# Attention and two feed-forward blocks in fp32: P*V of two heads on one half of the TensorE columns each, with the row sums taken by products of their own

## The chip, the cores and the metric

The kernel runs on one core of a Trainium2 chip. Its time is the device time of one execution in microseconds (us); of several runs the median counts. The engines are TensorE (PE, its weight loads shown as PEld), VectorE (DVE), ScalarE (ACT), GpSimd (POOL) and the DMA queues, which SyncE (SP), ACT and POOL issue.

## The reference

Three stages, all in fp32: attention with a soft cap on the scores, a feed-forward block with a sigmoid gate, and a second one with an RMS norm and a SiLU gate.

```
batch, n_heads, seq, head_dim = (2, 12, 448, 64)

def _attn_ref(q, k, v, cap):
    scores = q @ k.T / sqrt(64)
    scores = cap * tanh(scores / cap)
    attn = exp(scores - max(scores))
    attn = attn / (sum(attn) + 1e-09)
    return attn @ v

x = attention, as 896 tokens x 768
x = moe (x, w_in 768x2048, w_out 2048x768)
x = moe2(x, rms_g, w_gate and w_val 768x1536, w_out 1536x768)
```

The change touches the last two lines of the attention alone: the sum over the keys, its reciprocal, and the product with V.

## The kernel before, in words

**Pairs.** The 24 heads are worked off as 12 pairs (p, 0 to 11) of two heads each (e, 0 and 1). The 448 keys of a head are three chunks of 128 and a rest of 64. Scores are made transposed, with the keys on the partitions: for chunk c, `scores` (L296) writes a tile `s` with both heads side by side, six products of 64 contraction rows, three for each head, in the order e = 0, 1, 0, 1. The rests of both heads share one tile of 128 partitions (`scores_last`, L306, with the block weights `kb`). `exps` (L318, L319) applies tanh and exp on ACT and leaves the unnormalized P of a chunk in SBUF: `tt` (128x896, both heads) for a chunk and `tl` (128x448) for the rests. No maximum is subtracted.

**P*V and the sums.** `pv(p, e)` (L330) runs once for each head: four fp32 products (three chunks and the rest), each with 128 weight columns. 64 of these are the head's V, and the other 64 are ones, which POOL writes into the tiles `vn` and `ve` at the start. So one PSUM bank receives the output on one half of its partitions and the row sum, repeated, on the other. DVE copies the bank into `z` (L336; for the last pair ACT does, L338).

**The reciprocals.** `sums` cuts one row of each head's `z` over 64 partitions by a DMA (L344, into `rs`, 128x7), `recips` inverts these 128x7 numbers on DVE (L350) and writes them to DRAM (L353, `recs`), and `spread` reads them back over all partitions (L368, `r`, 128x448). All three are DMAs that POOL issues. For the last three pairs the DMA from `z` is issued by SP, and the spreading is done on chip, with a product by a pattern `spr` on DVE (L358) and a product with block weights `blk` on PE (L372). `norm_mul` (L379, once for each head, 64 partitions), `norm_hi` (L385; ACT for the last two pairs, L387) and `norm_lo` (L391) write the normalized output as a high and a low part into `x`, the feed-forward block's input.

**The order.** The program is written out by hand: each engine works in the order of the calls in the loop `for p in range(NPR + 1)`. Iteration p of it issues, on PE: scores of chunk 1 of pair p (L296); transposes of q and k of pair p + 1 (L264); P*V of head 0 of pair p - 1; scores of chunk 2 of p and of chunk 0 of p + 1; `scores_last`; P*V of head 1 of pair p - 1. Between these stand DVE's copy and split of the transposed q and k (L274, L275), POOL's copies into `kb` (L277), the reciprocals of pair p - 3, and the normalization of pair p - 4 (`normal`). `decode` sprinkles in three steps per iteration, from iteration 3 on, of the unpacking of the first feed-forward weights (on DVE L137, L143, L149, L163; on ACT L125, L129, L133, L158): one step behind the first P*V, two behind the normalization. After the loop the first feed-forward block begins (`ffn1`, products at L541 to L543). Its first three columns of 18 products use tokens of the first batch alone (pairs 0 to 5); the tokens of pairs 6 to 11 are read first by the 128x512 products that follow.

**PSUM.** The attention has two tiles `s` of two banks, one `t` of two banks for the transposes, and two banks `v`, which warm-up, `scores_last` and P*V take in turn: whoever takes one waits until the reader of the use before last is done.

Of the kernel before, what the change touches and what calls it, by code (L numbers as in the profile page):

```python
# [18 lines left out]
def attn_moe_kernel(  # L19
# [14 lines left out]
    nc = tc.nc  # L34
# [22 lines left out]
    spr = keep.tile([128, S], F32, name="spr")  # L57
# [119 lines left out]
    def attention():  # L177
        with ExitStack() as actx:
# [15 lines left out]
            vns = [ap_.tile([128, NC, 12 - 4 * i, D], F32, name=f"vn{i}", bufs=1) for i in range(2)]  # L194
            ves = [ap_.tile([128, 3 - i, 4, D], F32, name=f"ve{i}", bufs=1) for i in range(2)]
            kbs = [ap_.tile([128, 2, 128], F32R, name=f"kb{i}", bufs=1) for i in range(2)]

            def constants():
                for r in raws:
                    for nm in "kq":  # L200
                        nc.gpsimd.memset(r[nm][64:128, NC], 0.0)
                for kb in kbs:
                    nc.gpsimd.memset(f(kb), 0.0)
                for vn, ve in zip(vns, ves):
                    for c in range(NC):
                        nc.gpsimd.memset(vn[:, c, 1::2], 1.0)
                    for e in range(2):
                        nc.gpsimd.memset(ve[half[e], :, 1 + e], 1.0)
                        nc.gpsimd.memset(ve[half[1 - e], :, 2 * e:2 * e + 2], 0.0)

            def late_constants():
                for e in range(2):
                    nc.gpsimd.memset(spr[half[e]], 1.0)
                    for lo in (True, False):

                        nc.gpsimd.affine_select(
                            out=spr[half[e]], in_=spr[half[e]], pattern=[[1 if lo else -1, S]],
                            compare_op=ALU.is_ge, fill=0.0, base=0 if lo else 6,
                            channel_multiplier=-7 if lo else 7,
                        )  # L220
# [3 lines left out]
            xs, pt, zt, nr = {}, {}, {}, {}  # L224
# [12 lines left out]
            def load_v(g):  # L237
                p0, n = GROUPS[g]
                for c in range(NC):
                    nc.sync.dma_start(  # L240
                        out=vns[g % 2][:, c, 0:4 * n:2], in_=rows(v, p0, n, c).rearrange("h p d -> p h d")
                    )
                for e in range(2):
                    nc.sync.dma_start(
                        out=ves[g % 2][half[e], 0:n, 3 * e], in_=rows(v, p0, n, NC)[e:2 * n:2].rearrange("h p d -> p h d")
# [76 lines left out]
            def pv(p, e):  # L322

                g, i = place[p]
                h = 2 * i + e
                ps = ps_v.tile([128, 512], F32, tag="v", name="v")
                for c in range(NC + 1):

                    w = vns[g % 2][:, c, 2 * h - e:2 * h - e + 2] if c < NC else ves[g % 2][:, i, 2 * e:2 * e + 2]
                    nc.tensor.matmul(  # L330
                        out=ps[:, 0:S], lhsT=w.rearrange("p h d -> p (h d)"),
                        rhs=pt[p, c][:, e] if c < NC else pt[p, c], start=(c == 0), stop=(c == NC),
                    )
                zt[p, e] = zrp.tile([128, S], F32, tag="z", name="z", bufs=7)
                if p < NPR - 1:
                    nc.vector.tensor_copy(zt[p, e], ps[:, 0:S])  # L336
                else:
                    nc.scalar.activation(out=zt[p, e], in_=ps[:, 0:S], func=AF.Copy)  # L338

            def sums(p):  # L340
                nr[p] = zrp.tile([128, S // 64], F32, tag="rs", name="rs", bufs=3)
                for e in range(2):

                    (nc.gpsimd if p < NPR - 3 else nc.sync).dma_start(  # L344
                        out=nr[p][half[e]], in_=zt[p, e][64 - 64 * e:65 - 64 * e, :].rearrange("o (a n) -> o a n", a=64)
                    )

            def recips(p):
                rs = nr[p]
                nc.vector.reciprocal(out=rs, in_=rs)  # L350
                if p < NPR - 3:
                    d = dram.tile([2, S], F32, tag="recs", name="recs")
                    nc.gpsimd.dma_start(out=d.rearrange("e s -> (e s)").rearrange("(p n) -> p n", p=128), in_=rs)  # L353
                    nr[p] = d
                else:

                    r = zrp.tile([128, S], F32, tag="r", name="r", bufs=3)
                    nc.vector.tensor_tensor(  # L358
                        out=r.rearrange("p (a n) -> p a n", n=7), in0=spr.rearrange("p (a n) -> p a n", n=7),
                        in1=rs.unsqueeze(1).to_broadcast([128, 64, 7]), op=ALU.mult,  # L360
                    )
                    nr[p] = r

            def spread(p, bank=None):
                d = nr[p]
                if p < NPR - 3:
                    r = zrp.tile([128, S], F32, tag="r", name="r", bufs=3)
                    nc.gpsimd.dma_start(out=r, in_=d.unsqueeze(1).to_broadcast([2, 64, S]))  # L368
                    nr[p] = (r, r)
                else:  # L370
                    o = bank()
                    nc.tensor.matmul(out=o[:, 0:S], lhsT=blk, rhs=d, start=True, stop=True)  # L372
                    nr[p] = (o[:, 0:S], d)

            def norm_mul(p):
                by, r = nr[p]
                for e in range(2):
                    z = zt.pop((p, e))
# [473 lines left out]
```

## Time and profile before

| | |
|---|---|
| Median of 3 runs | 640.83 us (640.73 to 641.07) |
| Span of the profiled execution, first to last instruction | 639.5 us |
| PE, DVE, ACT, POOL busy, share of the span | 98%, 69%, 63%, 13% |
| Attention, to the first feed-forward product | 138.5 us |

The profile lists each execution of an instruction with its engine, line and tiles. "Span" runs from the first to the last instruction; the time of a run holds some 1.3 us more. No other time of the profiled execution is shown. A busy PE is not a PE at its peak, since records of products overlap: the distance between starts tells more than their length. L296 is line 296 of the kernel before, which is printed above.

### The profile page before, as it was taken

Reading aid. Unit: us, or ns where it says so; the run is one execution under the profiler, and the core shown is the slowest. Engines: PE = TensorE matmul, PEld = TensorE weight load, DVE = VectorE, ACT = ScalarE, POOL = GpSimd, SP = SyncE. Lnnn points to the kernel's source line nnn. Section 1 sums busy time; section 2 is a strip of 40 time slices with the busy share of each in tenths; the row PEclk is TensorE's granted clock in tenths of the full one; section 3 lists DMA queues with packets and bytes.
Section 4 is the critical chain, followed back from the end, with each engine's and each line's share of the span. In section 5 each row is a group of like instructions: output and inputs, shape, how many; then the busy total and the mean of one; then the engine's idle time right before and its main releaser. Section 6 shows DMA issues by size and latency. Waiting matters only on the chain.

```text
span 639.5 us, 8022 instructions
## 1 busy us (share of the span) xinstructions
PE 627.8 (98%) x3076; PEld 529.1 (83%) x3076; DVE 439.0 (69%) x561; ACT 400.4 (63%) x534; POOL 81.1 (13%) x127
## 2 busy tenths in 40 slices
PE   7999999988999999999999999999999999999997
PEld 4655555557888899899898888999998899999997
DVE  2235677667777554467678889999378887588842
ACT  4869878828777654677767666668345676355500
POOL 5322233200000000000002220310012200023100
PEclk9999999999999999999999999999999999999999
DMA  6836433133423442233333423434323234232012
GB/s 136 184 97 149 120 79 97 31 87 89 134 100 121 127 147 82 68 99 106 132 109 98 127 73 102 144 100 148 99 63 134 101 100 148 58 137 102 1 64 109
DMA packets 85925, 67.18 MB, mean 105 GB/s; under 512 B 39924, under 2 KB 83206, under 8 KB 85888
## 3 DMA queue, kind: packets, MB, share of 16 engines
q1 hardware_dynamic: 80720, 64.28, 33.1%
q0 software_dynamic: 4208, 2.16, 1.3%
q8 instruction: 24, 0.39, 0.3%
q10 hardware_dynamic: 960, 0.23, 0.2%
q14 instruction: 13, 0.11, 0.1%
HBM read 63.80 MB, written 2.78 MB: 104 GB/s over the span
## 4 chain that ended last, share of the span: by engine, by line
PE 92%; DVE 3%; DMA 3%; issue 1%; SPq 1%; ACT 1%; POOL 0%; ACTq 0%; DVEq 0%; POOLq 0%
PE b L543 21%; PE b L542 21%; PE b L541 21%; PE b L746 14%; PE v L330 8%; PE s L296 4%; PE t L264 2%; PE v L306 1%; DMA r<-recs 1%; DMA q<-in_q 1%; DVE r L379 1%; SPq L235 1%; DMA rs<-z 0%; DVE x L274 0%; DVE x L391 0%
## 5 line engine op out<-in xcount | busy, mean ns | idle before, releaser
L541 PE MATMUL b<-x,ring 128*128 128x512 f32 (+1 forms) x480 | 174.4, 363 | 0.0
L543 PE MATMUL b<-x,ring 128*128 128x512 f32 (+1 forms) x480 | 174.2, 363 | 0.0
L542 PE MATMUL b<-x,ring 128*128 128x512 f32 (+1 forms) x480 | 174.0, 363 | 0.0
L542 PEld LDWEIGHTS b<-x,ring 128*128 128x128 f32 x480 | 90.1, 188 | 10.2 <-issue 0.4
L541 PEld LDWEIGHTS b<-x,ring 128*128 128x128 f32 x480 | 90.1, 188 | 10.1 <-issue 0.4
L543 PEld LDWEIGHTS b<-x,ring 128*128 128x128 f32 x480 | 90.1, 188 | 9.4
L746 PE MATMUL b<-ring,uA 128*128 128x384 f32 x504 | 87.8, 334 | 0.0
L746 PEld LDWEIGHTS b<-ring,uA 128*128 128x128 f32 x504 | 87.4, 188 | 0.0
L137 DVE SCALAR_TENSOR_TENSOR dec<-raw,dec 128x768 uint32<-128x768 uint32 x68 | 69.7, 1024 | 24.6 <-ACT dec L133 23.2
L143 DVE SCALAR_TENSOR_TENSOR dec<-raw,dec 128x768 uint32<-128x768 uint32 x68 | 73.1, 1076 | 1.1
L543 PE MATMUL b<-g,ring 128*128 128x384 f32 (+1 forms) x192 | 70.0, 365 | 0.0
L542 PE MATMUL b<-g,ring 128*128 128x384 f32 (+1 forms) x192 | 69.8, 364 | 0.0
L541 PE MATMUL b<-g,ring 128*128 128x384 f32 (+1 forms) x192 | 69.6, 362 | 0.0
L163 DVE TENSOR_TENSOR ring<-dec,ring 128x768 fp32r<-128x768 f32 x68 | 66.7, 983 | 3.6 <-ACT ring L158 3.6
L158 ACT ACTIVATE ring<-dec 128x768 fp32r<-128x768 f32 x68 | 56.7, 834 | 16.7 <-DVE dec L149 8.5
L149 DVE SCALAR_TENSOR_TENSOR dec<-raw,dec 128x768 uint32<-128x768 uint32 x68 | 64.9, 954 | 1.3
L129 ACT ACTIVATE dec<-dec,edge 128x768 f32<-128x768 f32 x68 | 63.4, 932 | 0.9
L125 ACT ACTIVATE dec<-raw 128x768 f32<-128x768 f32 x68 | 60.8, 894 | 0.6 <-DVE ring L163 0.5
L133 ACT ACTIVATE dec<-dec 128x768 f32<-128x768 f32 x68 | 57.3, 842 | 1.5
L330 PE MATMUL v<-tt,vn 128*128 128x448 f32 x144 | 58.2, 540 | 0.0
L714 POOL TENSOR_TENSOR a<-a,gg 128x512 f32<-128x512 f32 (+1 forms) x18 | 29.7, 1648 | 188.6 <-DVE gg L707 188.6
L318 ACT ACTIVATE tt<-s,tsc 128x896 f32<-128x896 f32 x36 | 35.9, 997 | 19.5 <-PE s L296 19.5
(103 smaller groups left out, 666.7 us busy)
## 6 DMA issues: line engine op xcount, KB each, us to landing
raw<-in_moe_w_out SPq DMA_DIRECT2D x20, 768.0 KB, 4.2
raw<-in_moe_w_in SPq DMA_DIRECT2D x16, 768.0 KB, 4.6
raw<-in_moe_w_gate SPq DMA_DIRECT2D x12, 768.0 KB, 4.2
raw<-in_moe_w_val SPq DMA_DIRECT2D x12, 768.0 KB, 4.2
raw<-in_moe_w_out SPq DMA_DIRECT2D x8, 512.0 KB, 3.8
out<-oacc SPq DMA_DIRECT2D x6, 384.0 KB, 2.3
raw<-in_moe_w_out SPq DMA_DIRECT2D x8, 256.0 KB, 3.6
r<-recs POOLq DMA_DIRECT2D x9, 224.0 KB, 7.7
```

Of the source, the lines that this page charges most:

```text
L125: nc.scalar.activation(out=f(d), in_=f(r[:, :, 1]), func=AF.Square, scale=2.0 ** 15)
L129: nc.scalar.activation(out=f(d), in_=f(d), func=AF.Sign, bias=edge)
L133: nc.scalar.activation(out=f(d), in_=f(d), func=AF.Relu, scale=2.0 - 2.0 ** -23)
L137: nc.vector.scalar_tensor_tensor(out=d, in0=hi, scalar=3, in1=d, op0=ALU.logical_shift_left, op1=ALU.bitwise_and)
L143: nc.vector.scalar_tensor_tensor(out=d, in0=hi, scalar=0xC0000000, in1=d, op0=ALU.bitwise_and, op1=ALU.bitwise_or)
L149: nc.vector.scalar_tensor_tensor(out=d, in0=lo, scalar=29, in1=d, op0=ALU.logical_shift_right, op1=ALU.bitwise_or)
L163: nc.vector.tensor_tensor(out=t[:, 1], in0=f(d), in1=f(t[:, 0]), op=ALU.subtract)
L330: nc.tensor.matmul(out=ps[:, 0:S], lhsT=w.rearrange("p h d -> p (h d)"), rhs=pt[p, c][:, e] if c < NC else pt[p, c], start=(c == 0), stop= ...
L541: nc.tensor.matmul(out=wide(o, b), lhsT=w0, rhs=x0, start=first, stop=False)
L542: nc.tensor.matmul(out=wide(o, b), lhsT=w0, rhs=x1, start=False, stop=False)
L543: nc.tensor.matmul(out=wide(o, b), lhsT=w1, rhs=x0, start=False, stop=last)
L746: nc.tensor.matmul(out=os_[t][n][:, 0:HW], lhsT=uA[xi][:, i, tok], rhs=w[:, wi, n * HW:(n + 1) * HW], start=(i == 0 and xi == 0 and wi == ...
```

## The change

Line numbers of the kernel after are those of its own text (its P*V is L314 and L318, its products for the sums L341 and L345).

- `outputs(p)` takes the place of the two `pv`. The tiles `vn` and `ve` hold V alone. For each of three chunks there are two products of 64 weight columns: head 0 into PSUM partitions 0 to 63, head 1 into 64 to 127 of the same bank. The rest of both heads is one product of 128 columns with block weights `ve`. One copy (L324) moves the bank to `z`; the last pair's is ACT's.
- `add_two` (DVE, L330) and `add_third` (POOL, L333) add the three tiles `tt` of a pair into `ts` (128x896). `sums` multiplies `ts` with ones, 64 columns for each head, and `tl` with `blk`, into one more bank. The last pair has no `ts`: its three `tt` are multiplied one by one.
- Up to pair 8 DVE copies the sums' bank to `sc` (L350), and the way over the DMAs is that of before. For pairs 9, 10 and 11 DVE inverts the bank, 128x448, straight from PSUM (L358). `spr`, its pattern, `bank`, the product with `blk` behind it and SP's DMAs are gone.
- `norm_mul` is one instruction of 128 partitions instead of two of 64. `normal(9)` moves to the end of iteration 11, `normal(10)` into iteration 12's end, behind `sums`; pair 11 is normalized in the first feed-forward step.

```diff
-            def pv(p, e):
+            def outputs(p):
                 g, i = place[p]
-                h = 2 * i + e
                 ps = ps_v.tile([128, 512], F32, tag="v", name="v")
-                for c in range(NC + 1):
-                    w = vns[g % 2][:, c, 2 * h - e:2 * h - e + 2] if c < NC else ves[g % 2][:, i, 2 * e:2 * e + 2]
-                    nc.tensor.matmul(
-                        out=ps[:, 0:S], lhsT=w.rearrange("p h d -> p (h d)"),
-                        rhs=pt[p, c][:, e] if c < NC else pt[p, c], start=(c == 0), stop=(c == NC),
-                    )
-                zt[p, e] = zrp.tile([128, S], F32, tag="z", name="z", bufs=7)
+                for c in range(NC):
+                    for e in range(2):
+                        nc.tensor.matmul(
+                            out=ps[half[e], 0:S], lhsT=vns[g % 2][:, c, 2 * i + e], rhs=pt[p, c][:, e],
+                            start=(c == 0), stop=False, skip_group_check=True,
+                        )
+                nc.tensor.matmul(
+                    out=ps[:, 0:S], lhsT=ves[g % 2][:, i].rearrange("p h d -> p (h d)"), rhs=pt[p, NC],
+                    start=False, stop=True, skip_group_check=True,
+                )
+                zt[p] = zrp.tile([128, S], F32, tag="z", name="z", bufs=5)
...
+            def add_two(p):
+                ts_[p] = ap_.tile([128, 2, S], F32, tag="ts", name="ts")
+                nc.vector.tensor_tensor(out=ts_[p], in0=pt[p, 0], in1=pt[p, 1], op=ALU.add)
+
+            def add_third(p):
+                nc.gpsimd.tensor_tensor(out=ts_[p], in0=ts_[p], in1=pt[p, 2], op=ALU.add)
+
             def sums(p):
...
+                ps = ps_v.tile([128, 512], F32, tag="v", name="v")
+                streams = [ts_[p]] if p < NPR - 1 else [pt[p, c] for c in range(NC)]
+                for n, t in enumerate(streams):
+                    for e in range(2):
+                        nc.tensor.matmul(
+                            out=ps[half[e], 0:S], lhsT=f(ones)[:, half[e]], rhs=t[:, e],
+                            start=(n == 0), stop=False, skip_group_check=True,
+                        )
+                nc.tensor.matmul(
+                    out=ps[:, 0:S], lhsT=blk, rhs=pt[p, NC], start=False, stop=True, skip_group_check=True
+                )
+                if p < NPR - 3:
+                    sc = zrp.tile([128, S], F32, tag="sc", name="sc", bufs=2)
+                    nc.vector.tensor_copy(sc, ps[:, 0:S])
+                    nr[p] = zrp.tile([128, S // 64], F32, tag="rs", name="rs", bufs=3)
...
+                else:
+                    nr[p] = zrp.tile([128, S], F32, tag="r", name="r", bufs=3)
+                    nc.vector.reciprocal(out=nr[p], in_=ps[:, 0:S])
...
                 if 3 <= p < NPR:
                     recips(p - 3)
+                if 1 <= p < NPR:
+                    add_third(p - 1)
+                if 3 <= p < NPR:
                     spread(p - 3)
                 if p >= 1:
-                    pv(p - 1, 0)
-                if p == NPR:
-                    recips(p - 2)
-                    spread(p - 3, bank)
+                    outputs(p - 1)
...
                 if p >= 4:
                     normal(p - 4)
-                if p == NPR:
-                    normal(p - 3)
-                if p == NPR - 1:
-                    recips(p - 2)
+                if p < NPR - 1:
+                    add_two(p)
                 if p >= 1:
                     decode(2 if p > 2 else 0)
-                    pv(p - 1, 1)
                     sums(p - 1)
-                if p == 0:
-                    late_constants()
+                if p >= NPR - 1:
+                    normal(p - 2)
```

On PE, one iteration of the loop from the transposes (`t`) on; `v<-tt` and `v<-tl` are P*V, `s` the scores, `v<-x,kb` the rest's scores. Before:

```order
L264 MATMUL t<-ident,k_104 128x128 x4
L264 MATMUL t<-ident,q_105 128x128 x4
L330 MATMUL v<-tt,vn_106 128x448 x3
L330 MATMUL v<-tl,ve_108 128x448
L296 MATMUL s<-x 128x448 x12
L306 MATMUL v<-x,kb_110 128x448 x3
L330 MATMUL v<-tt,vn_106 128x448 x3
L330 MATMUL v<-tl,ve_108 128x448
L296 MATMUL s<-x 128x448 x6
```

and after the change, the same iteration (`v<-ts,ones` and `v<-tl,blk` are the sums):

```order
L250 MATMUL t<-ident,k_103 128x128 x4
L250 MATMUL t<-ident,q_104 128x128 x4
L314 MATMUL v<-tt,vn_105 64x448 x6
L318 MATMUL v<-tl,ve_107 128x448
L282 MATMUL s<-x 128x448 x12
L292 MATMUL v<-x,kb_110 128x448 x3
L341 MATMUL v<-ts,ones 64x448 x2
L345 MATMUL v<-tl,blk 128x448
L282 MATMUL s<-x 128x448 x6
```

All of the pair's P*V now stands ahead of the scores; the place of the second head's P*V holds the sums.

On POOL, one iteration; `kb` is the copy that the next `scores_last` needs, the rest is the way of the reciprocals. Before:

```order
L277 CAST kb_111<-x 64x2x64 x2
L353 DMA recs<-rs 128x7
L368 DMA r<-recs 128x1x448
L344 DMA rs<-z 64x1x7 x2
```

and after:

```order
L263 CAST kb_110<-x 64x2x64 x2
L364 DMA recs<-rs 128x7
L333 TENSOR_TENSOR ts<-ts,tt 128x896
L369 DMA r<-recs 128x1x448
L353 DMA rs<-sc 64x1x7 x2
```

The addition stands behind `kb` and the first DMA of the reciprocals, and ahead of the second; PE's sums wait for it.

On DVE after the change, one iteration with two decode steps (L142, L148), from the split of the next pair's q and k on:

```order
L260 CAST x<-t 128x896
L261 TENSOR_TENSOR x<-t,x 128x896
L362 RECIPROCAL rs<-rs 128x7
L324 COPY z<-v 128x448
L142 SCALAR_TENSOR_TENSOR dec<-raw,dec 128x768
L372 TENSOR_TENSOR r<-z,r 128x448
L377 CAST x_65<-r 128x448
L383 TENSOR_TENSOR x_66<-r,x_65 128x448
L330 TENSOR_TENSOR ts<-tt 128x896
L148 SCALAR_TENSOR_TENSOR dec<-raw,dec 128x768
L350 COPY sc<-v 128x448
```

Before it were the same without `ts`, with two multiplications of 64 partitions for the one at L372, and with the second head's `z` in the place of `sc`.

## Rows read from the trace of the kernel before

**Rows 1.** The page, parts 1 and 2: the span, and each engine's busy time and share.

```profile
span 639.5 us, 8022 instructions
PE 627.8 (98%) x3076; PEld 529.1 (83%) x3076; DVE 439.0 (69%) x561; ACT 400.4 (63%) x534; POOL 81.1 (13%) x127
```

**Rows 2.** The chain of waits, one pair: start us, duration us, engine, tile, line, instructions.

```profile
60.39 1.02 PE t L264 x8
61.42 3.01 PE v L330 x8
64.43 1.42 PE s L296 x12
65.84 0.81 PE v L306 x3
66.66 3.01 PE v L330 x8
69.66 0.81 PE s L296 x6
70.47 1.02 PE t L264 x8
```

**Rows 3.** The scores' line, 64.3 to 66 us: duration ns min/median/max of the records.

```profile
L296 PE MATMUL s<-x x12: 358/363/468, 64.4 to 65.5; 64*128 64x448 f32 x12
```

**Rows 4.** Busy time in one pair: start:end, length, PE, PEld, DVE, ACT, POOL, PEclk, DMA.

```profile
60.33:70.40 10.07, 10.07 (x48) 5.80 (x46) 7.53 (x11) 7.93 (x10) 3.00 (x6) 1.00 0.37 106
```

**Rows 5.** The timeline of DVE and POOL, same pair: start us, us, instruction, idle before.

```profile
61.52 1.09 DVE L274 CAST x<-t 128x896 fp32r<-128x896 f32 x1 [1.27 <-PE t L264]
62.65 1.09 DVE L275 TENSOR_TENSOR x<-t,x 128x896 fp32r<-128x896 f32 x1
63.91 0.63 POOL L277 CAST kb<-x 64x128 fp32r<-64x128 f32 x2 [2.83 <-DVE rs L350]
64.46 0.62 DVE L336 COPY z<-v 128x448 f32<-128x448 f32 x1 [0.62 <-PE v L330]
64.51 0.55 POOL L353 DMA_DIRECT2D recs<-rs  x1
65.00 0.95 DVE L143 SCALAR_TENSOR_TENSOR dec<-raw,dec 128x768 uint32<-128x768 uint32 x1
66.09 1.25 DVE L379 TENSOR_TENSOR r<-z,r 64x448 f32<-64x448 f32 x2
67.81 0.63 DVE L391 TENSOR_TENSOR x<-r,x 128x448 fp32r<-128x448 f32 x1
```

**Rows 6.** Groups on POOL by shape: additions of two tiles in SBUF; busy us, mean ns.

```profile
L638 POOL TENSOR_TENSOR sqs<-sqs,sq 128x512 f32<-128x512 f32 x5 | 6.5, 1297 | 16.7 <-ACT sq L634 16.7
L638 POOL TENSOR_TENSOR sqs<-sqs,sq 128x384 f32<-128x384 f32 x5 | 5.2, 1037 | 223.2 <-ACT sq L634 223.2
```

**Rows 7.** The timeline in the second feed-forward block: POOL's product beside DVE.

```profile
420.04 0.96 DVE L137 SCALAR_TENSOR_TENSOR dec<-raw,dec 128x768 uint32<-128x768 uint32 x1
420.23 1.92 POOL L714 TENSOR_TENSOR a<-a,gg 128x512 f32<-128x512 f32 x1 [4.51 <-DVE gg L707]
421.03 1.94 DVE L143 SCALAR_TENSOR_TENSOR dec<-raw,dec 128x768 uint32<-128x768 uint32 x1
```

**Rows 8.** Groups on DVE by shape: reciprocals of wide tiles.

```profile
L694 DVE RECIPROCAL rr<-rr 128x512 f32<-128x512 f32 x1 | 3.3, 3337 | 0.0
L694 DVE RECIPROCAL rr<-rr 128x384 f32<-128x384 f32 x1 | 2.6, 2552 | 0.2 <-ACT rr L691 0.2
```

**Rows 9.** PE's timeline from the last transposes to the first product that needs pairs 6 to 11.

```profile
110.69 0.33 PE L264 MATMUL t<-ident,k 128*128 128x128 f32 x1
...
137.98 1.02 PE L372 MATMUL t<-r,blk 128*128 128x448 f32 x2 [2.56 <-DVE r L379]
...
147.02 0.99 PE L372 MATMUL b<-r,blk 128*128 128x448 f32 x2 [1.77 <-ACT dec L129]
...
150.82 0.33 PE L543 MATMUL b<-x,ring 128*128 128x384 f32 x1
150.99 0.39 PE L541 MATMUL b<-x,ring 128*128 128x512 f32 x1
```

More of the change, by code (lines that the diff above doesn't have):

```diff
@@ L240, in load_v @@
                     nc.sync.dma_start(
-                        out=vns[g % 2][:, c, 0:4 * n:2], in_=rows(v, p0, n, c).rearrange("h p d -> p h d")
+                        out=vns[g % 2][:, c, 0:2 * n], in_=rows(v, p0, n, c).rearrange("h p d -> p h d")
                     )
@@ L244, in load_v @@
                     nc.sync.dma_start(
-                        out=ves[g % 2][half[e], 0:n, 3 * e], in_=rows(v, p0, n, NC)[e:2 * n:2].rearrange("h p d -> p h d")
+                        out=ves[g % 2][half[e], 0:n, e], in_=rows(v, p0, n, NC)[e:2 * n:2].rearrange("h p d -> p h d")
                     )
@@ L335, in pv @@
                 if p < NPR - 1:
-                    nc.vector.tensor_copy(zt[p, e], ps[:, 0:S])
+                    nc.vector.tensor_copy(zt[p], ps[:, 0:S])
                 else:
-                    nc.scalar.activation(out=zt[p, e], in_=ps[:, 0:S], func=AF.Copy)
-            def sums(p):
[L341 to L346, printed above, removed]
+                    nc.scalar.activation(out=zt[p], in_=ps[:, 0:S], func=AF.Copy)
@@ L350, in recips, with spread @@
                 nc.vector.reciprocal(out=rs, in_=rs)
[L351 to L364, printed above, removed]
-                d = nr[p]
[L366 to L373, printed above, removed]
-            def norm_mul(p):
-                by, r = nr[p]
-                for e in range(2):
-                    z = zt.pop((p, e))
-                    nc.vector.tensor_tensor(out=r[half[e]], in0=z[half[e]], in1=by[half[e]], op=ALU.mult)
-                nr[p] = r
+                nr[p] = dram.tile([2, S], F32, tag="recs", name="recs")
+                nc.gpsimd.dma_start(out=nr[p].rearrange("e s -> (e s)").rearrange("(p n) -> p n", p=128), in_=rs)
+            def spread(p):
+                d = nr[p]
+                nr[p] = zrp.tile([128, S], F32, tag="r", name="r", bufs=3)
+                nc.gpsimd.dma_start(out=nr[p], in_=d.unsqueeze(1).to_broadcast([2, 64, S]))
+            def norm_mul(p):
+                nc.vector.tensor_tensor(out=nr[p], in0=zt.pop(p), in1=nr[p], op=ALU.mult)
             def norm_hi(p):
@@ L421, in normal @@
                 norm_lo(p)
-            spare = []
-            def bank():
-                if not spare:
-                    spare.append(ps_t.tile([128, 2, 512], F32, tag="t", name="t"))
-                    return spare[0][:, 0]
-                return spare[0][:, 1]
             nc.vector.reciprocal(out=tsc, in_=capt)
@@ L481, in attention, with rest @@
             decode(len(early))
-            spread(NPR - 2, bank)
-            return recips, spread, norm_mul, norm_hi, norm_lo
-    def rest(recips, spread, norm_mul, norm_hi, norm_lo):
+            return norm_mul, norm_hi, norm_lo
+    def rest(norm_mul, norm_hi, norm_lo):
         with ExitStack() as fctx:
```

32 lines of the change are left out of this document (11 added, 21 removed).

## The prediction

> **What bounds the kernel now.** I read the page first: PE is busy for 627.8 of 639.5 us, all others for less than 70% [rows 1]. Then the chain of waits, in the stretch of one pair of heads: it stays on PE through the whole pair, 10.08 us from one set of transposes to the next, and no other engine enters it [rows 2]. So in the attention PE's own work sets the pace, and the change has to be costed there first. DVE has 2.5 us of each 10.07 free, ACT 2.1, POOL 7 [rows 4]. The third place is the end of the attention, in PE's timeline: PE waits 2.56 us for DVE's `r`, and 1.77 us for the last one, and issues three products with `blk` of 0.75 us each, before the first product that needs pairs 6 to 11 at 150.99 [rows 9].
>
> Of one profiled execution I have the span, 639.5 us; the median of the runs is 640.83. I take the 1.3 us around the span as unchanged and add my differences to 640.83. Some 0.2%, or 1.3 us, can be told from no change.
>
> **PE, per pair.** One head's P*V is eight records in 3.01 us: each of four fp32 products is two records of 0.376 us [rows 2]. In place of 16 records per pair come: P*V of six half-wide products (12 records) and one wide one (2), sums of two half-wide (4) and one wide (2). What a half-wide record costs hangs on whether the two column halves work at the same time. No row shows column halves. The nearest is the scores' products, which use one half of the rows each: 12 records of 0.36 us stand in a piece of 1.42 us [rows 2, 3], so two run side by side, at 0.2 us per couple: (1.42 - 0.81) / 3. The bounds are therefore 12 times 0.376 (all halves in couples) and 20 times 0.376 (none).
>
> There is a middle. The two records of one product use the same half and must follow each other. If records also start in the program's order, the second record of head 0 runs beside the first of head 1, and so on: 12 half records take 7 steps and 4 take 3, together with the wide ones 14 steps, 5.26 us against 6.02. The Trainium skill, "TensorE: Matmul & The Clock Gate", section "Part 3: Packing small matmuls", says that column tiles do run together and that products start strictly in program order. The rows agree on row halves; by both statements together the middle case holds, by the first alone the 12 steps.
>
> Going over between halves and full width costs as well: 12 score records take 1.42 us and 6 take 0.81, which leaves 0.2 us in each piece over 0.2 per couple, and 0.2 in the 0.81 us of the three products of L306 [rows 2]. The change adds four such passages per pair (into and out of the halves, for P*V and for the sums): 0.8 us at this price, nothing at the least. So PE's pair is 10.08 - 0.75 + 0.8 = 10.12 us in the middle case, 9.37 in couples, 12.37 one by one.
>
> **DVE and POOL, per pair.** Times from here count from the transposes at 60.39 [rows 2]. DVE loses one multiplication of 0.62 and gains `add_two`; a two-input 128x896 operation took 1.09 (L275). One copy stays a copy (`sc`) [rows 5]. POOL gains a 128x896 addition: 1297 ns for 512 columns and 1037 for 384 give 2.03 ns a column, so 2.1 us [rows 6]. Where it stands matters. POOL is done with `kb` at 4.15 and with the first DMA at 4.67 [rows 5], so the addition runs from 4.7 to 6.85. PE comes to the sums at 1.02 + 2.83 + 0.95 + 1.42 + 0.81 = 7.03. That just fits: the addition is hidden with 0.2 us to spare, and any lag of DVE is a lag of the sums, since `kb` hangs on DVE's split.
>
> And DVE will lag. POOL's two-input product and DVE's two-input operations exclude each other [rows 7]: POOL came while L137 ran and took 1.92 instead of 1.30, and L143 came while POOL ran and took 1.94 instead of 0.96. The Trainium skill, "GPSIMD Engine Reference", section "8. Key points", has it so: the two share SBUF interfaces when DVE has two SBUF inputs; the trace agrees, with these 1.94 us. So DVE's next two-input operation after the copy of `z` (P*V ends at 4.8, the copy at 5.5) waits until 6.85. Then, with one decode step behind the normalization: normalization 1.73 (66.09 to 68.44 less one multiplication), `add_two` 1.09, decode 0.95, `sc` 0.62: 11.3. The next split is due at 10.12 + 1.13 = 11.25. No lag. With two decode steps (L143 ahead, 0.95): 12.2, a lag of 1 us, of which PE's next sums see 0.8. By the program's order pairs 5, 7, 9 and 10 have two steps, 4, 6 and 8 one, 1 to 3 none. For iterations 1 to 9 the sum is: 1 to 3, 0.05 us each; 4 to 9, twice 0.9 us of lag and six times 0.05; +2.3 us. In couples PE is faster, but from iteration 5 on the same loop over DVE and POOL sets the pace: -1.9 for 1 to 3, +1.8 after, together -0.1.
>
> **The end.** From the last transposes (110.69) to 150.99 it takes 40.3 us before [rows 9]. After: the wide reciprocal costs (3337 - 2552) / 128 = 6.13 ns a column, 2.94 us for 448 [rows 8], three times, where 0.2 us stood. In iteration 10 DVE, 1.1 us behind, takes L142 (to 6.5) before POOL adds (to 8.7), normalizes (10.4), adds (11.5), decodes (12.45) and inverts pair 9 (15.4). Behind that stand the small reciprocal, POOL's DMA (16.15) and the addition of pair 10 (18.3); only then come sums(10) on PE, to 20.6. PE has waited some 2 us for it. P*V of pair 11 (3.78) and its sums in three streams (3.78) end at 28.2. The 54 products of the first three columns at 0.17 each (150.82 to 150.99) take 9.4: 37.6. Pairs 10 and 11 must be normalized by then, plus the 2.8 us of products that come ahead of pair 10's: DVE ends with pair 11 at some 39, and has 2 us to spare. So the end gains 2.7 us: no holes for `r`, no `blk` products, but a new hole for DVE. In couples it gains 3.5.
>
> Edits without a cost: fewer POOL memsets at the start (POOL is not in the chain), SP's six small DMAs, `vn` of half the size.
>
> **Sum.** Middle case +2.3 - 2.7 = -0.4 us; couples -0.1 - 3.5 = -3.6. I take -1.5, nearer to the middle case, which the order of records favours: **639.3 us**, range of this case 636 to 642.
>
> **Rivals.** *The halves take turns* (slower). If column halves do not overlap, PE's pair is 12.37 us, iterations 1 to 9 cost 9 times 2.3 = 20.7, the end 2.7: 664 us, or 653 if the passages are free. It decides as soon as 16 steps are passed; for it speaks that no row shows column halves in fp32, against it the row halves' clean couples. *DVE and POOL get along*: if POOL's addition holds up no DVE operation, no lag arises; the middle case is then -4.3, couples -9: 632 to 637. Rows 7 speak against it. *The addition is long*: at the 1.92 us for 512 columns of rows 7, 896 take 3.3 us, and sums come 1.1 us late in each of iterations 3 to 9: +8, 646 us. It holds if POOL, too, has to wait for DVE each time; DVE mostly waits for POOL here, since POOL starts while DVE is in PSUM work.
>
> **Numbers.** Forecast 0.5, halves in turn 0.17, getting along 0.2, long addition 0.13. Faster by over 0.2% (under 639.5): half of the forecast and nearly all of the third, 0.44. Within: the rest of the forecast mostly, 0.23. Slower: 0.17 and 0.13 and a little of the forecast, 0.33. For 8 in 10 the range holds forecast, getting along and most of the long addition: 631 to 649; the turns stay outside. The forecast's own range is 636 to 642.
>
> **What would show it.** In the profile after: starts of the two heads' P*V records about 0.38 us apart with four records in 1.1 to 1.2 us (couples: both within some ns; in turn: 1.5 us); PE waits for POOL's `ts` ahead of the sums in pairs with two decode steps, under 1.2 us; DVE decode operations of 1.9 to 2.2 us beside POOL's `ts`; `ts` near 2.1 us; three DVE reciprocals of 2.9 us and PE waiting for `ts` before the last but one sums. I am wrong if P*V and sums of a pair take over 7 us of PE, if `ts` takes over 2.8, or if the first product for pairs 6 to 11 waits for `x`.

## The result and the profile after

The changed kernel takes **633.98 us** in the median (632.75 to 634.54, 4 runs), against 640.95 (640.73 to 641.65, 4 runs) for the kernel before, run beside it: a ratio of 0.9878, interval 0.9863 to 0.9893. That is 7 us or 1.2% less. 639.3 was forecast with a range of 631 to 649, and 636 to 642 for the forecast's own case. The sign and the wide range hold; the time lies below the forecast's own range.

The head of the page answers to [rows 1]:

```profile
span 632.3 us, 8124 instructions
PE 616.2 (97%) x3126; PEld 511.0 (81%) x3126; DVE 462.2 (73%) x555; ACT 399.2 (63%) x533; POOL 99.5 (16%) x122
```

PE lost 11.6 us of busy time and the span 7.2, so PE waits more than it did. DVE is busy for 23 us more than before [rows 1].

One pair in the chain of waits (start us, us, engine, tile, line, records), beside [rows 2]:

```profile
28.72 1.02 PE t L250 x8
29.74 2.40 PE v L314 x12
32.15 0.95 PE v L318 x2
33.09 1.43 PE s L282 x12
34.53 0.81 PE v L292 x3
35.33 0.90 PE v L341 x4
36.23 0.95 PE v L345 x2
37.18 0.80 PE s L282 x6
37.99 1.04 PE t L250 x8
```

This pair takes PE alone 9.27 us, against 10.08 in [rows 2]. The twelve half-wide records of P*V take 2.40 us, which is six steps of 0.376 and 0.15; with the wide rest and the sums (0.95, 0.90, 0.95) they make 5.2 us where two pieces of 3.01 stood. Both heads' records start together, as the answer on L314 shows for the first 60 ns of this piece in a later pair (number of records, duration ns min/median/max, first and last start in us):

```profile
L314 PE MATMUL v<-tt,vn x2: 590/590/590, 58.0 to 58.0; 128*64 128x448 f32 x2
```

So the column halves run in **couples**: the lower bound of the prediction, and not its middle case.

Not all pairs are that short. PE's timeline, rows of two pairs that follow each other (start, us, instruction, in brackets idle before and who ended it):

```profile
57.00 0.65 PE L250 MATMUL t<-ident,k 128*128 128x128 f32 x4
...
63.95 0.97 PE L341 MATMUL v<-ts,ones 128*64 128x448 f32 x4 [0.27 <-POOL ts L333]
...
66.62 0.66 PE L250 MATMUL t<-ident,k 128*128 128x128 f32 x4
...
75.13 0.97 PE L341 MATMUL v<-ts,ones 128*64 128x448 f32 x4 [1.83 <-POOL ts L333]
...
77.78 0.66 PE L250 MATMUL t<-ident,k 128*128 128x128 f32 x4
```

The first takes 9.62 us and the second 11.16: PE waits for POOL's addition ahead of the sums. T(p) is the start of pair p's transposes. From T(2) at 19.04 to T(11) at 108.60 the nine distances are 9.61, 9.27, 9.53, 9.55, 9.62, 11.16, 9.56, 11.60 and 9.65 us. Why POOL is late shows in DVE's timeline (first block) and POOL's (second), in answer to [rows 5]:

```profile
62.03 2.69 DVE L142 SCALAR_TENSOR_TENSOR dec<-raw,dec 128x768 uint32<-128x768 uint32 x1
...
68.97 1.08 DVE L260 CAST x<-t 128x896 fp32r<-128x896 f32 x1
...
72.51 0.63 DVE L372 TENSOR_TENSOR r<-z,r 128x448 f32<-128x448 f32 x1 [0.74 <-DMA r<-recs]
73.17 2.16 DVE L377 CAST x<-r 128x448 fp32r<-128x448 f32 x1
```

```profile
61.78 2.11 POOL L333 TENSOR_TENSOR ts<-ts,tt 128x896 f32<-128x896 f32 x1
...
71.31 0.64 POOL L263 CAST kb<-x 64x128 fp32r<-64x128 f32 x2 [0.91 <-DVE rs L362]
71.92 0.57 POOL L364 DMA_DIRECT2D recs<-rs  x1
72.56 2.52 POOL L333 TENSOR_TENSOR ts<-ts,tt 128x896 f32<-128x896 f32 x1
```

While POOL adds at 61.78, DVE's decode step takes 2.69 us instead of 0.95 [rows 5]. With a second step to do, DVE copies the next pair's transposes only at 68.97, 2.35 us after they began (1.13 in [rows 5]). POOL's `kb` and DMA, and the addition behind them, follow that lag. The second addition, 72.56 to 75.08, is what PE waits for.

The end, in answer to [rows 8] and [rows 9]: PE first, then DVE's wide reciprocals.

```profile
108.60 0.65 PE L250 MATMUL t<-ident,k 128*128 128x128 f32 x4
...
126.02 0.97 PE L341 MATMUL v<-ts,ones 128*64 128x448 f32 x4 [1.74 <-POOL ts L333]
...
143.99 0.39 PE L521 MATMUL b<-x,ring 128*128 128x512 f32 x1
```

```profile
119.99 2.95 DVE L358 RECIPROCAL r<-v 128x448 f32<-128x448 f32 x1
...
128.33 2.95 DVE L358 RECIPROCAL r<-v 128x448 f32<-128x448 f32 x1
...
137.12 2.95 DVE L358 RECIPROCAL r<-v 128x448 f32<-128x448 f32 x1
```

From T(11) to the first 128x512 product it takes 35.4 us, against 40.3 in [rows 9]. The account of the span, in us:

| stretch | before | after | difference | forecast, in couples |
|---|---|---|---|---|
| to T(2) | 19.70 | 19.04 | -0.66 | 0 |
| T(2) to T(5) | 30.55 | 28.41 | -2.14 | -1.9 |
| T(5) to T(11) | 60.44 | 61.15 | +0.71 | +1.8 |
| T(11) to the first 128x512 product | 40.30 | 35.39 | -4.91 | -3.5 |
| from there to the end | 488.5 | 488.3 | -0.2 | 0 |
| sum | 639.5 | 632.3 | -7.2 | -3.6 |

The first line can't be put down to the change: in the profiles of the changed kernel and of its versions below, T(2) stands between 19.0 and 19.8 us (20.65 in the one with more DMAs at the start). Nor is the distance from T(2) to T(3) the same each time. It is 9.61 us here and 10.33 in the last run below, whose program is the same up to there, so it is partly luck that the second line agrees with its forecast.

### The profile page after: what moved, and what is told of

It reads as the page before. It is cut to its first block, busy times and chain, and to the rows that moved or that the text cites. A ratio compares the mean times of both kernels' runs of the same rounds, so it can differ in the third digit from the quotient of the medians.

```text
span 632.3 us, 8124 instructions
## 1 busy us (share of the span) xinstructions
PE 616.2 (97%) x3126; PEld 511.0 (81%) x3126; DVE 462.2 (73%) x555; ACT 399.2 (63%) x533; POOL 99.5 (16%) x122
## 3 DMA queue, kind: packets, MB, share of 16 engines
q0 software_dynamic: 4208, 2.16, 1.3%
## 4 chain that ended last, share of the span: by engine, by line
PE 86%; DVE 4%; DMA 3%; POOL 3%; issue 3%; SPq 1%; POOLq 0%
PE b L523 21%; PE b L522 21%; PE b L521 21%; PE b L724 14%; PE v L314 2%; POOL ts L333 2%; PE s L282 1%; PE v L341 1%; DMA r<-recs 1%; PE t L250 1%; PE v L345 1%; DMA recs<-rs 1%; DVE x L260 1%; DMA q<-in_q 1%; PE v L318 1%
## 5 line engine op out<-in xcount | busy, mean ns | idle before, releaser
L136 DVE SCALAR_TENSOR_TENSOR dec<-raw,dec 128x768 uint32<-128x768 uint32 x68 | 71.5, 1052 | 26.6 <-ACT dec L132 25.4
L142 DVE SCALAR_TENSOR_TENSOR dec<-raw,dec 128x768 uint32<-128x768 uint32 x68 | 74.9, 1102 | 1.1
L162 DVE TENSOR_TENSOR ring<-dec,ring 128x768 fp32r<-128x768 f32 x68 | 68.5, 1008 | 3.6 <-ACT ring L157 3.6
L148 DVE SCALAR_TENSOR_TENSOR dec<-raw,dec 128x768 uint32<-128x768 uint32 x68 | 64.9, 955 | 1.4
L616 POOL TENSOR_TENSOR sqs<-sqs,sq 128x384 f32<-128x384 f32 (+1 forms) x10 | 11.7, 1172 | 231.8 <-ACT sq L612 231.8
```

What stands on the lines that cost most here:

```text
L136: nc.vector.scalar_tensor_tensor(out=d, in0=hi, scalar=3, in1=d, op0=ALU.logical_shift_left, op1=ALU.bitwise_and)
L142: nc.vector.scalar_tensor_tensor(out=d, in0=hi, scalar=0xC0000000, in1=d, op0=ALU.bitwise_and, op1=ALU.bitwise_or)
L148: nc.vector.scalar_tensor_tensor(out=d, in0=lo, scalar=29, in1=d, op0=ALU.logical_shift_right, op1=ALU.bitwise_or)
L162: nc.vector.tensor_tensor(out=t[:, 1], in0=f(d), in1=f(t[:, 0]), op=ALU.subtract)
```

## The experiments

Two theories were open. **Couples:** the gain is PE's, because the halves overlap whatever the order of the records; its rival was the middle case, in which the order of the program counts. And for the pairs of 11 us: **the exclusion** of DVE and POOL against **the reciprocals' way over the DMAs**.

### The heads one after the other

```diff
-                for c in range(NC):
-                    for e in range(2):
+                for e in range(2):
+                    for c in range(NC):
                         nc.tensor.matmul(
```

> The changed kernel with the two loops of P*V exchanged: three products of head 0, then three of head 1. Theory (halves of the columns run side by side only where they are neighbours in the program's order): the twelve records take 10 to 12 steps of 0.376 us instead of 6, P*V 3.8 to 4.5 us instead of 2.4, PE's pair 10.8 to 11.4 us and the kernel 643 to 650 us. Rival (PE finds the other half wherever it stands): 2.4 us and no change of time.

Measured: 636.97 us, ratio 0.9937 (0.9919 to 0.9954), each pair from T(3) on 10.06 us, without a wait of PE. Neither expectation holds. The chain's row for P*V, and the answer on L314 for the stretch around 62.05 us:

```profile
61.31 3.21 PE v L314 x12
```

```profile
L314 PE MATMUL v<-tt,vn x3: 539/539/590, 61.7 to 62.0; 128*64 128x448 f32 x3
```

P*V takes 3.21 us, which is eight steps and the passage, between six and twelve. A record of 590 ns is the first of a half (as in the couples above, 590/590). The one here starts at 62.05, beside the third record of head 0, which is the first of its second product. So head 1's first product begins ahead of head 0's third, though the program has it behind. The start is not in the program's order across the halves: PE takes work for the idle half from a little further down its list, but not at once from behind all of the first head's. The order of the two loops is worth 0.8 us a pair; alternating heads gives all of the overlap.

### Full-width products instead of halves

P*V of both heads still goes to one bank, but each V stands beside 64 columns of zeros.

```diff
-                            out=ps[half[e], 0:S], lhsT=vns[g % 2][:, c, 2 * i + e], rhs=pt[p, c][:, e],
-                            start=(c == 0), stop=False, skip_group_check=True,
+                            out=ps[:, 0:S],
+                            lhsT=vns[g % 2][:, c, 4 * i + 2 * e:4 * i + 2 * e + 2].rearrange("p h d -> p (h d)"),
+                            rhs=pt[p, c][:, e], start=(c == 0 and e == 0), stop=False, skip_group_check=True,
```

> Edit: P*V alone as full-width products whose other half of the columns is zero, both heads still in one bank; sums, additions and reciprocals as in the changed kernel. Theory (the gain is the halves' overlap): P*V takes 14 records one after the other, 5.0 us less what the rest piece's last record hides, in place of 2.4 + 0.95, so a pair takes 9.55 + 2.1 - 0.4 for two passages = 11.2 us; with ten pairs and the end 645 to 652 us. Rival (the gain comes from what went away elsewhere: small DMAs, multiplications, spread products at the end): at most 3 us above the changed kernel, about 637.

Measured: 650.56 us, ratio 1.0137 (1.0112 to 1.0161); pairs of 11.16 to 11.18 us from T(3) on, without a wait.

```profile
56.17 4.51 PE v L319 x12
60.68 0.75 PE v L324 x2
```

As the theory had it. P*V costs 5.26 us instead of 3.35, the pair 1.9 us more. Of the 16.6 us above the changed kernel, some 1.6 lie ahead of T(2), where this version has more DMAs and memsets, 11.9 between T(2) and T(11), and 3.0 from T(11) to the first 128x512 product. The overlap of P*V's halves is what turns the change from slower into faster; everything else in it, taken together, costs time.

### The rests in halves as well

```diff
-                nc.tensor.matmul(
-                    out=ps[:, 0:S], lhsT=blk, rhs=pt[p, NC], start=False, stop=True, skip_group_check=True
-                )
+                for e in range(2):
+                    nc.tensor.matmul(
+                        out=ps[half[e], 0:S], lhsT=blk[:, half[e]], rhs=pt[p, NC],
+                        start=False, stop=True, skip_group_check=True,
+                    )
...
```

(and so for `ve`)

> The changed kernel, with the 64 keys of the rest also multiplied in column halves, two products of 64 columns in the place of one of 128, for P*V and for the sums. That takes away two of the four new passages between halves and full width. Theory (a passage costs 0.2 us, a couple of halves as much as one full record): 0.4 us less on PE per pair; it shows in the first two pairs and at the end, while between them the sums wait for POOL as before: 632 to 633 us. Rival (the halves' records of the rest do not run side by side, or passages are free): same or up to 0.75 us per product more.

Measured: 632.57 us, ratio 0.9869 (0.9851 to 0.9887), which by the time alone can't be told from the change (0.9863 to 0.9893). Two of the chain's rows:

```profile
31.61 0.75 PE v L319 x4
...
35.55 0.75 PE v L347 x4
```

Both rest pieces fall from 0.95 to 0.75 us: the passage from halves to full width, 0.2 us, is gone, and four half-wide records cost what two wide ones do. PE's share of a pair becomes 8.9 us. It shows where nothing is late: the pairs take 9.02 and 8.94 at first, but 9.3 to 10.3 from T(4) on, since PE now waits for POOL in all of them.

### The third addition earlier in POOL's order

```diff
+                if 1 <= p < NPR:
+                    add_third(p - 1)
                 if p + 1 < NPR:
                     turn(p + 1)
                     split_kq(p + 1)
                 if 3 <= p < NPR:
                     recips(p - 3)
-                if 1 <= p < NPR:
-                    add_third(p - 1)
-                if 3 <= p < NPR:
                     spread(p - 3)
```

> The changed kernel with one call moved: POOL's third addition stands ahead of the transposes of its iteration, so that it runs while DVE reads PSUM (split of q and k) and not beside the decode and the normalization. Theory (POOL's addition and DVE's operations with two SBUF inputs exclude each other, and the lag that comes of it makes the pairs of 11.2 and 11.6 us): decode operations of 2.6 us fall to 1, all pairs from the fourth on take 9.3 to 9.7 us, and since the addition of pair 10 no longer stands behind the wide reciprocal of pair 9, PE's hole of 1.7 us ahead of the last but one sums goes too: about 630 us, 4 below the changed kernel. Rival (the two long pairs come from DVE's own work or from the late landing of the spread reciprocals): under 1 us gained, long pairs stay.

Measured: 632.40 us, ratio 0.9864 (0.9838 to 0.9890): no gain over the change that can be told. POOL now adds while DVE works from PSUM, six pairs in a row take 9.26 us, and then one takes 13.01. Around it: DVE, POOL's queue, the chain, and busy time in a window (start:end, length, PE, PEld, DVE, ACT, POOL, PEclk, DMA share, GB/s).

```profile
85.96 0.62 DVE L372 TENSOR_TENSOR r<-z,r 128x448 f32<-128x448 f32 x1 [3.26 <-DMA r<-recs]
```

```profile
77.82 0.82 POOL L369 DMA_DIRECT2D r<-recs  x1 [5.75 <-DMA recs<-rs]
```

```profile
93.26 1.42 PE v L292 x3
```

```profile
80.00:100.00 20.00, 18.30 (x91) 8.73 (x92) 14.39 (x19) 14.26 (x17) 10.91 (x15) 0.91 0.13 31
```

POOL's DMA of `r` waits 5.75 us until `recs` has landed, lands itself only at 85.9, and DVE's multiplication holds up the rest of DVE's list, the copy of the next transposes at its end. PE stands still for 1.14 and 0.56 us, and then three products take 1.42 us that took 0.81: the granted clock, 0.91 over these 20 us, had gone to its lower level of 1.2 GHz for a while. One wait had gone and another took its place.

Both edits together (the rests in halves and the earlier addition):

> The two edits together, the early addition and the rest in halves. Theory: with DVE's lag gone PE sets the pace, and the 0.4 us per pair now count in each pair: 8.9 to 9.6 us per pair and 627 to 629 us. Rival (DVE, 9.8 us of work and waits in a pair with two decode steps, or ACT with 8.3 to 9.2 us sets the pace as soon as PE is faster): no more than 1 us below the early addition alone.

Measured: 632.38 us, ratio 0.9860 (0.9837 to 0.9884). Five pairs of 8.86 us, then 9.51 and 13.31, with the same multiplication waiting:

```profile
84.14 0.62 DVE L375 TENSOR_TENSOR r<-z,r 128x448 f32<-128x448 f32 x1 [3.21 <-DMA r<-recs]
```

### The third addition on DVE

```diff
-                nc.gpsimd.tensor_tensor(out=ts_[p], in0=ts_[p], in1=pt[p, 2], op=ALU.add)
+                nc.vector.tensor_tensor(out=ts_[p], in0=ts_[p], in1=pt[p, 2], op=ALU.add)
```

> Edit: the third addition of the sums on DVE instead of POOL, at its place in the program. Theory (the long pairs come in part from DVE and POOL shutting each other out, about 1 us in each pair with two decode steps, which is about what the addition costs on DVE): decode and add operations of DVE take 0.95 and 1.1 us throughout, the time is within 2 us of the changed kernel, 632 to 636. Rival (only the reciprocals' DMA way makes long pairs; the exclusion costs nothing as DVE has time): DVE's added 1.1 us per pair costs nothing either and the time is the same within 0.5 us, with the same long pairs. If DVE has no room, pairs become 10 us and the time is 638 or more.

Measured: 633.97 us, ratio 0.9876 (0.9852 to 0.9901). No DVE operation of the pairs is stretched any more, most pairs take 9.26 us, but two take 10.71 and 11.96 (and the first 10.52). From the list of waits between 50 and 110 us (total, times, longest):

```profile
POOL r L369 <- DMA recs<-rs: 26.5, 6, 5.4
DVE r L372 <- DMA r<-recs: 11.5, 6, 3.8
```

Without any exclusion the reciprocals' DMA way makes long pairs by itself. The equal median is made of two differences that cancel: T(2) to T(11) takes 88.74 us against 89.56, and the end 36.75 against 35.39. There PE waits 1.35 and 0.60 us for DVE, and behind that the granted clock falls: 0.91 from 120 to 140 us, against 1.00 in the changed kernel.

### Normalization one pair later

To give the DMA way more time, each pair is normalized one iteration later, with the two edits of the run with both and more buffers for `z` and `r`:

```diff
-                if p >= 4:
+                if 5 <= p < NPR - 1:
+                    normal(p - 5)
+                if p == NPR:
                     normal(p - 4)
...
+                if p == NPR - 1:
+                    normal(p - 5)
+                    normal(p - 4)
                 if p >= NPR - 1:
                     normal(p - 2)
```

> Edit: the third addition ahead of the next pair's split and the wide rest products in column halves, as in the run that joined the two, and besides each pair's normalization one pair later (pair p-5 in iteration p, the ones left over in the last two iterations). Theory (the DMA way of the reciprocals, about 6.5 us to gather and 6 to 8 us to spread, is what made one pair of 13.3 us there and left PE idle so that its granted clock fell): with one more pair of time no pair is longer than 9.6 us, the pairs take 8.9 us, the profile shows no stretch at half clock after the start, and the time is 626 to 629. Rival (DVE and ACT set the pace of the shorter pairs, and the long pair was only where the lag was paid): the time stays within 1 us of 632.4, and the long pair comes back with PE waiting for DVE's own work and not for a DMA.

Measured: 631.20 us, ratio 0.9833 (0.9809 to 0.9857). In the pairs the theory holds: the nine from T(2) on take 8.89 to 9.29 us, and none is long. But of the 4.6 us by which T(2) to T(11) is shorter than in the run with both, 2.0 are lost again behind T(11), where a wait of the same kind appears. DVE's rows, then PE's:

```profile
128.29 0.62 DVE L375 TENSOR_TENSOR r<-z,r 128x448 f32<-128x448 f32 x1 [2.22 <-DMA r<-recs]
...
131.78 2.95 DVE L361 RECIPROCAL r<-v 128x448 f32<-128x448 f32 x1
```

```profile
134.79 0.69 PE L528 MATMUL b<-x,ring 128*128 128x384 f32 x1 [4.42 <-DVE r L361]
```

Pair 8's normalization waits for its DMA, with the last wide reciprocal behind it on DVE. That reciprocal reads a PSUM bank, and PE's next piece of the feed-forward block starts only when it ends. After the 4.4 us PE runs at the lower clock for some us: the granted clock is 0.83 over 120 to 140 us.

### The last pair's reciprocal first

The edit, against the run before:

```diff
-                if p == NPR:
-                    normal(p - 4)
                 if p < NPR - 1:
                     add_two(p)
-                if p >= 1:
+                if 1 <= p < NPR:
                     decode(2 if p > 2 else 0)
+                if p >= 1:
                     sums(p - 1)
...
                 if p >= NPR - 1:
                     normal(p - 2)
+                if p == NPR:
+                    normal(p - 4)
```

> Edit: as the run with normalization one pair later, but in the last iteration the sums of the last pair and their reciprocal come first, then the normalizations of pairs 10 and 8, then the decode steps. Theory (there DVE's multiplication for pair 8 waited 2.2 us for the reciprocals' DMA and held up the last wide reciprocal, which frees the bank that the FFN's fourth row of products needs; PE stood still for 4.4 us and then ran at half clock for some us): the wide reciprocal ends near 129 us in place of 134.7, PE's wait of 4.4 us goes, no products of 0.32 us stand in the FFN's start, and the time falls by 5 to 6 us against that run, to 625 to 627. Rival (the products of the FFN then wait for the normalized columns of pairs 8, 10 and 11 instead): PE waits about as long, a little later, and the time falls by less than 2 us.

Measured: **624.11 us** (621.93 to 625.30, 5 runs), ratio 0.9714 (0.9694 to 0.9735), a little below the expected 625 to 627. This beats both kernels, by 2.9% and, through the two ratios, by 1.7%. The middle pairs and the two windows of the end, columns as above:

```profile
28.67:82.00 53.33, 53.33 (x321) 26.58 (x319) 35.97 (x48) 48.95 (x57) 29.29 (x39) 1.00 0.54 138
100.00:120.00 20.00, 17.85 (x92) 7.68 (x92) 16.59 (x18) 16.98 (x21) 8.97 (x10) 0.91 0.24 70
120.00:140.00 20.00, 20.00 (x107) 15.51 (x104) 16.54 (x22) 5.33 (x8) 0.81 (x1) 1.00 0.20 52
```

In six pairs PE doesn't wait at all, and the end is without a hole from 120 us on. What is left lies between 100 and 120: PE waits 1.85 us for POOL's addition ahead of sums(9). It is the reciprocals' way again: that addition stood in POOL's list behind the DMA of `r`, which had waited 4.92 us for `recs`.

### Only the later normalization

The same later normalization and the same end, but POOL's addition and the rests as the change has them:

```diff
-                if p >= 4:
-                    normal(p - 4)
+                if 5 <= p < NPR - 1:
+                    normal(p - 5)
...
```

> Edit: the changed kernel with the later normalization and the last iteration's order of the run before, but with POOL's addition and the rest products left where the change has them. Theory (in the changed kernel the two long pairs of 11.2 and 11.6 us are the reciprocals' DMA way, about 6.5 and 7.8 us, against DVE's order; POOL's addition shutting out DVE costs only some 0.3 us per pair): all pairs take 9.3 to 9.7 us, the time is 629 to 631, 3 to 5 us under the changed kernel. Rival (the lag from the mutual exclusion of DVE and POOL makes the long pairs, as the prediction had it for pairs with two decode steps): two or three pairs above 10.5 us stay, and the gain is under 2 us.

Measured: 633.44 us, ratio 0.9873 (0.9856 to 0.9890). The theory that I had put down here falls. DVE waits for no DMA in the pairs, and still two take 10.45 and 10.44 us, against 9.55 for the others:

```profile
62.02 2.65 DVE L142 SCALAR_TENSOR_TENSOR dec<-raw,dec 128x768 uint32<-128x768 uint32 x1
...
68.62 1.08 DVE L260 CAST x<-t 128x896 fp32r<-128x896 f32 x1
```

```profile
74.36 0.97 PE L341 MATMUL v<-ts,ones 128*64 128x448 f32 x4 [1.11 <-POOL ts L333]
```

This is the exclusion by itself. The decode step beside POOL's addition puts the copy of the next transposes 2.06 us behind their start at 66.56 (1.13 in [rows 5]), POOL's next addition follows, and each pair after two decode steps is 0.9 us longer than the others. The 0.3 us by which the others, at 9.55, lie above 9.26 are not the exclusion: there POOL adds undisturbed (61.73 to 63.85), and PE, faster by its couples, comes to the sums some 0.2 us before that.

The 2.1 us won from T(2) to T(11) were mostly lost again: from T(11) to the first 128x512 product it took 37.1 us, 1.7 more than in the changed kernel. Nearly all of this is the clock. PE waited 1.95 us ahead of the last but one sums (1.74 in the changed kernel), the granted clock was 0.91 from 120 to 140 us (1.00 there), and the last pair's P*V, in the chain, took

```profile
126.59 3.56 PE v L314 x12
```

instead of 2.40.

### The price of the wide reciprocals

```diff
-                    nc.vector.reciprocal(out=nr[p], in_=ps[:, 0:S])
+                    nc.vector.tensor_copy(nr[p], ps[:, 0:S])
```

> Edit: for pairs 9 to 11 the reciprocal of the sums (128x448 from PSUM) is a copy, so their inversion is left out. It prices the three wide reciprocals of 2.95 us at the end. Theory (DVE's way through the end, with the hole of 1.7 us of PE ahead of the last but one sums, is bounded by them): that hole closes, and the time falls by 1.5 to 2.5 us, to about 632. Rival (the reciprocals lie beside PE's work and the hole comes from POOL's addition alone): less than 0.5 us.

Measured: 631.85 us, ratio 0.9843 (0.9821 to 0.9864), some 2.1 us under the changed kernel. PE no longer waits ahead of the last but one sums:

```profile
123.57 0.97 PE L341 MATMUL v<-ts,ones 128*64 128x448 f32 x4
```

In the changed kernel that row has 1.74 us of idle time. From T(11) to the first 128x512 product it takes 33.6 us, 1.8 less than in the changed kernel. So the reciprocals cost the hole and little else: three times 2.3 us on DVE (2.95 less the copy's 0.62) come out as some 2 us.

This run says one thing more. Up to pair 8 its program is that of the changed kernel, and its two long pairs take 10.43 us each, where the changed kernel's took 11.16 and 11.60. The 10.4 is what the run with only the later normalization has too; the 0.7 and 1.2 us above it in the changed kernel's profile come mostly from the DMA way, and differ from one profile to the next. `r` landed after DVE was ready for it. In the first pair it came 0.74 us late (the row of 72.51 above), so that DVE's multiplication met POOL's addition, which took 2.52 us instead of 2.11. In the second, it came 1.08 us late and delayed DVE's list by that:

```profile
86.52 0.63 DVE L372 TENSOR_TENSOR r<-z,r 128x448 f32<-128x448 f32 x1 [1.08 <-DMA r<-recs]
```

## Why the prediction held, and which step of it failed

The time fell, as forecast, and lies in the wide range; the forecast's own case did not come about. **The step that failed** is "I take -1.5, nearer to the middle case, which the order of records favours". Its premise, that records of the two halves start in the program's order, was an inference from a rule with no row behind it, and it is wrong for them: couples start within one step, and with the heads in turn the second head's first product starts ahead of the first head's third. The Trainium skill, "TensorE: Matmul & The Clock Gate", section "Part 3: Packing small matmuls", has products start strictly in program order; here it differs from the measurement, and the measurement decides. Its other statement there, that column tiles run together, the trace confirms: 2.40 us for twelve records that take 4.51 us at full width. The rows of the kernel before could not decide it: in the scores' couples [rows 2, 3] each product is one record and the heads alternate, so the program's order gives couples there too.

- **PE per pair**: 9.37 in couples forecast, 9.27 measured. The four passages cost 0.7 us together, 0.8 forecast.
- **The exclusion** [rows 7]: right in kind, and in what it costs a pair. DVE's decode step takes 2.6 to 2.7 us beside POOL, where 1.9 to 2.2 was named; the pairs after two steps are 0.9 us longer by the exclusion alone, which is the forecast's figure. The Trainium skill, "GPSIMD Engine Reference", section "8. Key points", agrees; it names two SBUF inputs or a two-port mode of DVE as the condition, and L377, a copy with one input that took 2.16 us, would fall under the second, which no row here names.
- **The lag over T(5) to T(11)**: +1.8 forecast, +0.7 measured. I let the loop over DVE and POOL set the pace of every pair there, at the old 10.07 us for the short ones. The short ones took 9.55 to 9.65, PE's pace and 0.3; this is worth -1.9 over four. The two long ones took 0.8 more together than the forecast's 10.97 each, since the reciprocals' DMA way, which the forecast did not have, came on top; PE's waits there were 1.83 and 1.98 us, where under 1.2 was named.
- **The end**: -3.5 forecast, -4.9 measured. The hole ahead of the last but one sums was 1.74 us (2 forecast), each reciprocal 2.95 us (2.94), and `x` was ready in time. But POOL's last addition ended 17.4 us after T(11), not 18.3; the remaining 0.5 us are not traced.
- **To T(2)**: -0.66 us that belong to no part of the change.

With the table above, couples at the forecast's own prices give -3.6; the lag and the end bring -1.1 and -1.4, the first three pairs and the tail -0.4, T(2) -0.7: -7.2.

Of the **rivals**, *the halves take turns* is refuted by the couples. *The addition is long* is refuted too: `ts` took 2.1 to 2.5 us and did not reach 3.3. *DVE and POOL get along* named 632 to 637, and the time fell there, but for another reason: they do not get along. The wide range reached down to 631 for this rival's sake, so it is partly luck that it held the time. The rival's own sum was uneven as well: its middle case leaves out the 2 us hole at the end and its couples keep it; without the hole they give some -11, or 630 us.

## What to carry over

- When products of half the columns are packed, write them so that neighbours in the program use different halves: that alone was worth 0.8 us a pair here. And stay in halves: each way back to full width cost 0.2 us.
- A work list on an in-order engine that contains a wait for a DMA delays what stands behind it, even when it has nothing to do with it. Two causes of the same long pairs hid each other: taking away either one left the time the same within 2 us (in one run because a lower granted clock behind a wait took back what the pairs had won), and only removing both, with the rests in halves and the list at the end reordered, gave 10 us more.
- A rule that no row of the profile can decide should widen the range, not move the forecast. Here the nearest rows fitted both cases, and the forecast moved to the side of the rule, which was the wrong one.

## What had not been expected of the hardware

- PE starts a record of the idle column half ahead of earlier records of the busy one, from a few places down its list.
- The granted clock after a hole is not the same for each: after 1.83 and 1.98 us of waiting in the changed kernel (75.13 and 96.27) the products kept their length, and so they did after 2.15 us in the run with the rests in halves; after 1.85 us in the fastest version four records took 1.71 us in place of 0.97, with a granted clock of 0.91 over those 20 us, and after 1.95 us in the run with only the later normalization it fell as well. What decides stays open.
- Writing the 128x7 reciprocals to DRAM and reading them back over the partitions takes longer than PE's whole pair: 3.5 and 7.8 us in the median of the nine pairs, from issue to landing. One pair in the chain of the changed kernel:

```profile
71.92 6.49 DMA recs<-rs
...
78.69 7.81 DMA r<-recs
```
